# Routed attention and a cosine-gated MLP on one core: a remade instruction plan with fp32 turning of the first pairs, weights in sixteen paced pieces, and a last tile in halves

## Chip, cores, metric

One core of a Trainium2 chip. The time is the device time of one execution in microseconds (us). A run is called slow when it lies over 1.5% above the fastest of the same kernel on that chip; verdicts use the other runs, which are called fast.

## The reference, cut

```python
# q, k, v: (4, 8, 768, 64); centroids: (8, 16, 64); w_in: (512, 2048); w_out: (2048, 512)
q_assign = argmax(q_n @ c_n.T);  k_assign = argmax(k_n @ c_n.T)      # rows normalised
scores = where(q_assign[..., :, None] == k_assign[..., None, :], q @ k.T / 8, -1e9)
attn_out = softmax(scores) @ v
x = attn_out.transpose(0, 2, 1, 3).reshape(3072, 512)
h = x @ w_in
return (h * cos(h)) @ w_out                                           # (3072, 512) fp32
```

The kernel works on 16 pairs of heads (0 to 15, four for each batch entry). For each pair, scores of 80 rows (64 of q or k, 16 of the one-hot cluster) go through 9 exps. The MLP of a batch entry fills the time of later pairs. The first four pairs have no MLP work beside them. PE is TensorE, ACT ScalarE, DVE VectorE, POOL GpSimd and SP SyncE; "turned" means transposed, and a "move" is the 24 KB transfer that puts one-hot rows in their place.

## The kernel before

The program first collects operations with booked durations (`pl.add`), then a small planner simulates five engines and the DMA and emits each engine's instructions in the order found. On the chip each engine runs its own list strictly in that order. The planner's times exist only in the plan; what really holds an engine is a data dependence or a full buffer.

```python
# Plan.run, before: each queue's first transfer moves, and moving ones share the DMA by weights pk
heads = {}
for f in flying:
    heads.setdefault(f[0].ring, f)
moving = [f for f in heads.values() if f[2] <= t]
tot = sum(f[0].pk for f in moving)
...
# after routing: where a one-hot row goes. Pairs 0 and 1 (NHEAD = 2): turned by PE, copied by ACT and DVE.
if p < NHEAD:
    for hh in range(2):
        onehot_head(p, hh, ...)
else:
    onehot_pair(p, at + 5)      # turned, then four 24 KB moves: DMA copies into rows 64 to 79 of qkT
...
who, eng = ("SP", nc.sync) if p < HPB else ("POOL", nc.gpsimd)       # HPB = 4
pl.add(who, ..., lambda ...: eng.dma_start(out=turned(p, a, hh)[D:KDIM, :], in_=ohT[...]), ...)
...
def weight_ops():
    for ft in range(NFT):                                             # 4 loads of 512 KB
        pl.add("POOL", 0.6, lambda ft=ft: nc.gpsimd.dma_start(out=w_in_sb[:, ft, :], in_=w_in_r[ft]),
               -90 + 0.1 * ft, writes=[("w_in", ft)], ..., after=gate["hi", 2, 0], name="w_in")
    for f in range(0, NFPT, 4):                                       # 4 loads of 512 KB
        pl.add("POOL", 0.6, lambda f=f: nc.gpsimd.dma_start(out=w_out_sb[:, f:f + 4, :], ...),
               -50, writes=[("w_out", f // 4)], ..., after=gate["mv", 4], name="w_out")
    pl.add("SP", 0.45, lambda: nc.sync.dma_start(out=pace, in_=w_out_sb[0:1, NFPT - 1, 0:1]), 0,
           reads=[("w_out", 3)], writes=["pace"], ..., name="pace")
    gate["pace"] = (pl.ops[-1],)          # later loads and DMA transposes stand behind it on SP
```

The last line matters below. SP issues the loads of q, k and v and the large DMA transposes (`qkT<-stg`). Its two-byte transfer `pace` reads w_out, so SP **really waits** for the last w_out load, and everything behind it on SP's list waits too.

The softmax here doesn't subtract the row's maximum and nothing guards it: scores larger than these inputs give would overflow.

Of the kernel before, what the change touches and what calls it, by code (L numbers as in the profile page):

```python
# [19 lines left out]
class Op:  # L20
    __slots__ = ("eng", "occ", "lat", "work", "fn", "at", "nb", "deps", "outs", "left",
                 "take", "free", "table", "done", "idx", "name", "start", "ring", "pk", "urgent", "todo", "eta")


class Plan:
# [3 lines left out]
    HELD = 0.8  # L29
    OWN = {"PE": 0.0, "DVE": 0.11, "ACT": 0.0, "POOL": 0.08, "SP": 0.0}  # L30
    TABLE = 1.45
    urgent = False

# [5 lines left out]
    def add(self, eng, occ, fn, at, reads=(), writes=(), lat=0.13, work=0.0, nb=0.0, take=None,  # L39
            free=None, table=None, after=(), ring=None, pk=0.065, name="",  # L40
            urgent=False):
        o = Op()
        o.eng, o.occ, o.fn, o.at, o.lat, o.work, o.nb = eng, occ, fn, at, lat, work, nb
        o.take, o.free, o.table, o.name, o.ring, o.pk = take, free, table, name, ring, pk
# [18 lines left out]
    def run(self, stop=None):  # L63
# [9 lines left out]
        flying = []  # L73
# [14 lines left out]
        while n_left:  # L88
# [28 lines left out]
            for e in engines:  # L117
                if busy[e] > t or not ready[e] or any(
                        f[0].eng == e and f[0].pk < 0.02 and f[1] > self.HELD for f in flying):
                    continue  # L120
                back = []
                got = None
                while ready[e]:
                    item = heapq.heappop(ready[e])
                    o = item[2]
                    if o.take is not None and not free[o.take[0]]:
                        back.append(item)
                        continue
                    if (e == "DVE" or o.name == "warm") and any(x.at < o.at and x.eta < t + o.occ - 0.05 for x in soon[e]):
                        back.append(item)  # L130
                        break
                    got = o
                    break
# [8 lines left out]
                occ = o.occ  # L142
                if o.table is not None and o.table != table:
# [11 lines left out]
                if o.ring:  # L155
                    flying.append([o, o.work, t + min(occ, 0.45) + (1.1 if o.ring == "SW" else 0.8)])
# [3 lines left out]
            heads = {}  # L160
            for f in flying:
                heads.setdefault(f[0].ring, f)
            heads = list(heads.values())
            moving = [f for f in heads if f[2] <= t]
            tot = sum(f[0].pk for f in moving)
            when = [x for x in busy.values() if x > t] + [f[2] for f in heads if f[2] > t]
            when += [q[0][0] for q in (ends, coming) if q]
            for f in moving:
                when.append(t + f[1] * tot / f[0].pk)
                if f[1] > self.HELD and f[0].pk < 0.02:  # L170
                    when.append(t + (f[1] - self.HELD) * tot / f[0].pk)
# [6 lines left out]
            for f in moving:  # L178
                f[1] -= step * f[0].pk / tot
                if f[1] <= 1e-5:  # L180
                    heapq.heappush(ends, (t + 0.75, f[0].idx, f[0], False))
                    flying.remove(f)
        self.span = t
        return order


@with_exitstack
def kernel(
# [31 lines left out]
    NPE = 4  # L220
# [5 lines left out]

    NNAT, NSTG, NQK, NOH, NV, NE, NG, NO = 3, 2, 4, 2, 4, 4, 4, 3
    NACC = 4
    RT = 8
    BLOCKED = (HPB - 1,)  # L230
    NHEAD = 2
# [8 lines left out]
    ident = sb.tile([P, P], FP16, name="ident")  # L240
    oh_mul = sb.tile([P, 1], FP32, name="oh_mul")
# [25 lines left out]
    pl = Plan({"one": 4})  # L267
# [30 lines left out]
    def consts_ops():  # L298
        def mk_ident():
            make_identity(nc, ident)  # L300
        pl.add("POOL", 0.6, mk_ident, -90, writes=["ident"], name="ident")
# [21 lines left out]
    def warm_ops(n):  # L323
        for i in range(n):
            pl.add("PE", 0.43 if i < 8 else 0.216, lambda: nc.tensor.matmul(  # L325
                bank("warm"), lhsT=warm_z[:, 0:P], rhs=warm_z, start=True, stop=True),
                400 + i if i else -100, reads=["warm_z"] + ([] if i == 0 else [("warm", 0)]),
                writes=[("warm", i)], take=("one", "warm") if i == 0 else None,
                free="warm" if i == n - 1 else None, name="warm", lat=0.0)
# [8 lines left out]
    cn_s = sb.tile([HC, D], FP32, name="cn_s")  # L338
    cn_hl = sb.tile([HC, 2, 2, D], FP16, name="cn_hl")
    cside = sb.tile([P, H, 2, NCL], FP16, name="cside")  # L340

    def centroid_ops():
        V = nc.vector
        at = -120
        pl.add("ACT", 0.42, lambda: nc.scalar.dma_start(out=cn_raw, in_=centroids.rearrange("h c d -> (h c) d")),
               -149.9, writes=["cn_raw"], work=0.1, ring="ACT", name="ld cn")
        pl.add("DVE", 0.22, lambda: V.tensor_mul(cn_sq, cn_raw, cn_raw), at, ["cn_raw"], ["cn_sq"], name="cn")
        pl.add("DVE", 0.22, lambda: V.reduce_sum(out=cn_n2, in_=cn_sq, axis=AX.X), at, ["cn_sq"], ["cn_n2"], name="cn")
        pl.add("ACT", 0.2, lambda: nc.scalar.activation(out=cn_nrm, in_=cn_n2, func=AF.Sqrt), at,
               ["cn_n2"], ["cn_nrm"], table="sqrt", name="cn")  # L350
        pl.add("DVE", 0.15, lambda: V.tensor_scalar_add(cn_nrm, cn_nrm, 1e-6), at, ["cn_nrm"], ["cn_nrm2"], name="cn")
        pl.add("DVE", 0.16, lambda: V.reciprocal(cn_rcp, cn_nrm), at, ["cn_nrm2"], ["cn_rcp"], name="cn")
        pl.add("POOL", 0.3, lambda: nc.gpsimd.tensor_scalar(out=cn_s, in0=cn_raw, scalar1=cn_rcp, scalar2=ASCALE,
                                                    op0=ALU.mult, op1=ALU.mult), at, ["cn_rcp"], ["cn_s"], name="cn")
        wide = cn_s.rearrange("r (o d) -> r o d", o=1).to_broadcast([HC, 2, D])
        pl.add("POOL", 0.3, lambda: nc.gpsimd.tensor_copy(out=cn_hl[:, 0], in_=wide), at, ["cn_s"], ["cn_h"], name="cn")
# [505 lines left out]
```

## Time and profile before

| | us |
|---|---|
| median of 3 runs | 313.98 (313.61 to 314.23) |
| span of the profiled run | 312.2 |
| PE work at the measured peak rates | 287.7 |
| first exp starts / 36th exp (the last of pairs 0 to 3) ends | 15.84 / 54.28 |
| last matmul ends to end of span | 3.9 |

What to keep in mind for later are the transfers. These are rows of the page's sixth part for the kernel before: what is loaded, from which queue, how often, size of each, and the median time from issue to landing.

```profile
w_in_sb<-in_moe_w_in_dram POOLq DMA_DIRECT2D x4, 512.0 KB, 9.6
w_out_sb<-in_moe_w_out_dram POOLq DMA_DIRECT2D x4, 512.0 KB, 9.2
qkT<-ohT POOLq DMA_DIRECT2D x48, 24.0 KB, 2.9
```

And from its chain of waits (start, duration, what) the first large DMA transpose, that of pair 4, with no weight load in flight:

```profile
37.48 6.12 DMA qkT<-stg
```

Weights take 9 to 10 us to land in the median; w_in has landed by 29.7 and is first read at 53.7. The transpose takes 6.1 us (the later ones, also with no weight in flight, 5.6 to 9.8) and the one-hot moves 3 us, and PE stands behind both.

### The profile page before, as it was taken

What the parts mean: (1) busy time and instruction counts of PE and PEld (TensorE: products, weight loads), DVE (VectorE), ACT (ScalarE), POOL (GpSimd) and SP (SyncE); (2) the same over time, 40 slices, a digit from 0 to 9 for tenths busy, and PEclk for the clock granted to TensorE, in tenths of its full rate; (3) what the DMA queues carried; (4) which work ended last, traced back from release to release, by engine and by line L of the source; (5) the groups of instructions that cost most, each with busy time, mean ns of one, the idle gap of its engine ahead of it and who ended that gap; (6) DMA issues with size and microseconds to landing.
All of it is one profiled execution on the core that took longest, in us unless ns stands there. A gap on an engine that the chain in (4) does not pass through costs nothing.

```text
span 312.2 us, 7990 instructions
## 1 busy us (share of the span) xinstructions
PE 300.7 (96%) x3380; PEld 212.1 (68%) x3380; DVE 186.8 (60%) x362; ACT 213.7 (68%) x230; POOL 59.5 (19%) x114
## 2 busy tenths in 40 slices
PE   8899999999999799999999999999999999999995
PEld 3568877747785566788875567598866567776642
DVE  4789987513899467679872528677651123554431
ACT  5699999599249799875459996954479984533110
POOL 3793003401042232023132110032210100000000
PEclk9999999999999999999999999999999999999999
DMA  7897771797969999998545398972412202001012
GB/s 247 310 207 185 267 154 29 130 153 179 230 209 172 196 244 253 236 222 154 108 130 152 99 201 266 159 183 42 105 41 86 55 5 62 34 2 67 16 54 101
DMA packets 75254, 44.86 MB, mean 144 GB/s; under 512 B 56402, under 2 KB 71634, under 8 KB 75218
## 3 DMA queue, kind: packets, MB, share of 16 engines
q1 hardware_dynamic: 70706, 38.74, 50.2%
q0 software_dynamic: 4224, 5.38, 9.1%
q8 instruction: 26, 0.43, 0.6%
q10 hardware_dynamic: 288, 0.23, 0.2%
q14 instruction: 10, 0.08, 0.1%
HBM read 27.30 MB, written 6.29 MB: 108 GB/s over the span
## 4 chain that ended last, share of the span: by engine, by line
PE 76%; DMA 11%; ACT 6%; DVE 4%; POOL 1%; issue 1%; ACTq 0%; POOLq 0%; DVEq 0%
PE one L764 23%; PE big L728 23%; PE big L613 14%; PE one L679 8%; ACT e L619 5%; DMA qkT<-stg 5%; DMA w_out_sb<-in_moe_w_out_dram 3%; PE one L325 2%; DMA qkT<-ohT 2%; PE one L488 2%; PE one L460 2%; PE one L483 1%; DMA ohT<-oh 1%; DVE g L742 1%; POOL qkT L577 1%
## 5 line engine op out<-in xcount | busy, mean ns | idle before, releaser
L619 ACT ACTIVATE e<-big 128x1024 f16<-128x1024 f32 x144 | 139.6, 1022 | 12.0 <-PE big L613 10.9
L764 PE MATMUL one<-w_out_sb,g 128*128 128x512 f16 x384 | 108.3, 379 | 0.3 <-DMA w_out_sb<-in_moe_w_out_dram 0.3
L728 PE MATMUL big<-xt,w_in_sb 128*128 128x256 f16 x768 | 93.6, 272 | 0.8 <-DVE g L742 0.5
L736 ACT ACTIVATE cos_t<-big 128x1024 f16<-128x1024 f32 x48 | 49.1, 1023 | 65.8 <-PE big L728 63.7
L613 PE MATMUL big<-qkT 80*128 80x256 f16 (+1 forms) x396 | 85.2, 320 | 2.3 <-DMA qkT<-ohT 1.8
L728 PEld LDWEIGHTS <-w_in_sb 128*128 128x128 f16 x768 | 73.8, 98 | 17.1 <-issue 1.3
L742 DVE TENSOR_TENSOR g<-big,cos_t 128x1024 f16<-128x1024 f32 x48 | 58.6, 1222 | 32.3 <-ACT cos_t L736 32.0
L679 PEld LDWEIGHTS <-e 128*128 128x128 f16 x1080 | 45.7, 98 | 11.6
L764 PEld LDWEIGHTS <-g 128*128 128x128 f16 x384 | 36.3, 97 | 25.0 <-issue 0.7
L613 PEld LDWEIGHTS <-qkT 80*128 80x128 f16 x396 | 34.7, 97 | 25.5 <-DMA qkT<-ohT 2.3
L679 PE MATMUL one<-v_ext,e 128*128 128x65 f16 x1080 | 49.2, 194 | 0.0
L577 POOL DMA_DIRECT2D qkT<-ohT x48 | 23.7, 496 | 100.1 <-DMA ohT<-oh 46.2
L431 DVE SCALAR_TENSOR_TENSOR stg<-qk_nat,stg 128x384 f16<-128x384 f32 x64 | 34.9, 562 | 0.2
L771 DVE COPY o_sb<-one 128x512 f32<-128x512 f32 x24 | 16.5, 688 | 29.8 <-PE one L764 29.7
L396 POOL CAST v_ext<-v_nat 128x384 f16<-128x384 f32 x32 | 17.0, 562 | 75.7 <-DMA v_nat<-in_v_dram 75.6
L690 DVE RECIPROCAL recip<-one 128x6 f32<-128x6 f32 x30 | 5.8, 192 | 38.4 <-PE one L679 38.2
L427 DVE TENSOR_SCALAR stg<-qk_nat 128x384 f16<-128x384 f32 x48 | 16.5, 359 | 3.5 <-DMA qk_nat<-in_q_dram 2.8
L692 DVE TENSOR_TENSOR av_stage<-one,recip 128x384 f16<-128x384 f32 x30 | 16.6, 552 | 0.4
L502 DVE TENSOR_REDUCE csum<-one 128x192 f32<-128x384 f32 x24 | 12.9, 551 | 4.0 <-PE one L488 3.8
L488 PEld LDWEIGHTS <-qkT 128*128 128x128 f16 x288 | 10.9, 96 | 3.6 <-DMA qkT<-stg 1.6
L488 PE MATMUL one<-cside,qkT 128*128 128x32 f16 x288 | 11.5, 177 | 0.9 <-DMA qkT<-stg 0.9
L591 ACT ACT_TABLE_LOAD x9 | 11.5, 1283 | 0.2
(62 smaller groups left out, 129.7 us busy)
## 6 DMA issues: line engine op xcount, KB each, us to landing
v_nat<-in_v_dram SPq DMA_DIRECT2D x16, 384.0 KB, 4.5
out_dram<-o_sb SPq DMA_DIRECT2D x24, 256.0 KB, 2.2
qk_nat<-in_q_dram SPq DMA_DIRECT2D x15, 384.0 KB, 4.8
qk_nat<-in_k_dram SPq DMA_DIRECT2D x15, 384.0 KB, 5.3
w_in_sb<-in_moe_w_in_dram POOLq DMA_DIRECT2D x4, 512.0 KB, 9.6
w_out_sb<-in_moe_w_out_dram POOLq DMA_DIRECT2D x4, 512.0 KB, 9.2
qkT<-ohT POOLq DMA_DIRECT2D x48, 24.0 KB, 2.9
qk_nat<-in_q_dram SPq DMA_DIRECT2D x2, 192.0 KB, 3.1
```

Of the source, the lines that this page charges most:

```text
L396: pl.add("POOL", 0.5, lambda hh=hh: nc.gpsimd.tensor_copy(out=v_b[p % NV][:, hh, :, 0:D], in_=vnat_b[p % 2][:, hh]), (pair_at(p) - 2 if p ...
L431: pl.add("DVE", 0.476, lambda src=src, dst=dst: nc.vector.scalar_tensor_tensor(out=dst[:, :, 1, :], in0=src, scalar=ASCALE, in1=dst[:, :, ...
L488: nc.tensor.matmul(cs[:, a, t].rearrange("p i c -> p (i c)"), lhsT=turned(p, a, hh)[:, t * P:(t + 1) * P], rhs=cside[:, h].rearrange("p i ...
L577: pl.add(who, 0.61 if who == "SP" else 0.5, lambda hh=hh, a=a, r0=r0, eng=eng: eng.dma_start(out=turned(p, a, hh)[D:KDIM, :], in_=ohT[r0:r ...
L613: nc.tensor.matmul(big[i][:, x:x + w], lhsT=turned(p, 1, hh)[0:KDIM, jt * P:(jt + 1) * P], rhs=turned(p, 0, hh)[0:KDIM, col:col + w], star ...
L619: pl.add("ACT", 0.94, lambda i=i, c=c: nc.scalar.activation(out=e_b[p % (NE // 2)][:, c * CW:(c + 1) * CW], in_=big[i], func=AF.Exp, scale ...
L679: nc.tensor.matmul(av[:, i, :], lhsT=e_b[p % (NE // 2)][:, x:x + P], rhs=v_b[p % NV][:, hh, j, :], start=(j == 0), stop=(j == NT - 1))
L692: pl.add("DVE", 0.475, lambda av=av, r=r, hh=hh: nc.vector.tensor_tensor(out=av_t[:, :, hh, :], in0=av()[:, :, 0:D], in1=r.to_broadcast([P ...
L728: nc.tensor.matmul(bg[:, fi], lhsT=w_in_sb[:, ft, f * P:(f + 1) * P], rhs=xt_b[b % 2][:, ft, tg * TG:(tg + 1) * TG], start=(ft == 0), stop ...
L736: pl.add("ACT", 0.94, lambda bg=bg, cs=cs: nc.scalar.activation(out=cs, in_=bg, func=AF.Sin, bias=PI_HALF, scale=1.0), n, reads=[("big", i ...
L742: pl.add("DVE", 1.135, lambda bg=bg, cs=cs, c=c, slot=slot: nc.vector.tensor_tensor(out=g_b[slot][:, c * FQ:(c + 1) * FQ, :], in0=bg, in1= ...
L764: nc.tensor.matmul(bank(key), lhsT=g_b[slot][:, f, i * P:(i + 1) * P], rhs=w_out_sb[:, f, :], start=(f == 0), stop=(f == NFPT - 1))
```

## The change

The intent: start earlier (pairs 0 and 1 are turned while still fp32, and split into high and low halves on the way out of PSUM), let the planner see the DMA as one line that serves one transfer after another, search for better priorities in that planner (table `TUNE`, some 250 entries), bring the weights in 16 pieces of 256 KB that are let out only as earlier ones land, and shorten the end with a last tile in two halves.

```diff
 # the planner
-flying.append([o, o.work, t + min(occ, 0.45) + (1.1 if o.ring == "SW" else 0.8)])
+dma = max(dma, t + self.PRE[o.ring]) + o.work          # PRE: SP, ACT 1.5; SW (POOL) 0.85
+heapq.heappush(ends, (dma + self.POST, o.idx, o, False))   # POST 0.65
+TUNE = {'E0': -2.9, 'E1': -17.2, ... 'mv1.01': 'POOL', ... 'mv3.00': 'POOL', 'mv3.01': 'POOL', ...}
 ...
 # the head
-NPE = 4
-NHEAD = 2
+N32, NPE, NOT, NX, NSP = 2, 4, 5, 4, 5
+NHEAD = pick("nhead", 1, 1, 2)                         # TUNE has no "nhead": it is 1
+nc.tensor.transpose(out=bank(key)[:, u * P:(u + 1) * P], in_=nat[:, a, hh, 2 * u:2 * u + 2]..., identity=ident32)
+nc.scalar.mul(st[:, a, hh, 0], src(), ASCALE)          # split out of PSUM
-pl.add("ACT", 0.42, lambda: nc.scalar.dma_start(out=cn_raw, in_=centroids...), ...)
+pl.add("POOL", 0.6, lambda: nc.gpsimd.dma_start(out=cn_raw, in_=centroids...), ...)
 ...
 # one-hot moves
-who, eng = ("SP", nc.sync) if p < HPB else ("POOL", nc.gpsimd)
+who = pick(f"mv{p}.{hh}{a}", "SP" if p < NSP else "POOL", "SP", "POOL")
+eng = nc.sync if who == "SP" else nc.gpsimd
 ...
 # weights
+def weight_pieces(name, pieces, at, after):
+    for i, (key, dst, src) in enumerate(pieces):
+        if i > 1:
+            old = pieces[i - 2]
+            pl.add("POOL", 0.12, lambda old=old: nc.gpsimd.tensor_copy(out=pace, in_=old[1][0:1, 0, 0:1]), ...,
+                   reads=[old[0]], ..., name="pace")
+        pl.add("POOL", 0.77, lambda dst=dst, src=src: nc.gpsimd.dma_start(out=dst, in_=src), ..., work=1.5, bulk=True)
-pl.add("SP", 0.45, lambda: nc.sync.dma_start(out=pace, in_=w_out_sb[0:1, NFPT - 1, 0:1]), ...)
 # 'w_out_after': 'w_in' in TUNE: w_out follows w_in's last piece instead of pair 4's moves
 ...
 # the end
+cols = ((0, DM),) if (b, t) != (B - 1, NT - 1) else ((0, DM // 2), (DM // 2, DM))
```

(`...` marks cuts in the code. The whole diff is some 740 lines, mostly the remade head and the table.)

## The prediction

> **What bounds the kernel now.** I read the page first (engines, then groups), then the chain of waits, then busy time by stretches of 8 us, then the timeline of the first 20 us on each engine. Engine totals from the page:
>
> ```profile
> PE 300.7 (96%) x3380; PEld 212.1 (68%) x3380; DVE 186.8 (60%) x362; ACT 213.7 (68%) x230; POOL 59.5 (19%) x114
> PE 76%; DMA 11%; ACT 6%; DVE 4%; POOL 1%; issue 1%; ACTq 0%; POOLq 0%; DVEq 0%
> ```
>
> PE (TensorE) is busy 96%, but that alone does not say that it runs at its rate, because the ends of matmuls are modelled. So I took start-to-start times from merged pieces of the chain, where matmuls of one shape run back to back:
>
> ```profile
> 76.95 8.34 DMA qkT<-stg
> ...
> 139.03 3.49 PE big L728 x32
> ...
> 296.84 11.45 PE one L764 x53
> 308.32 0.69 DVE o_sb L771
> ```
>
> 512 columns: 11.45/53 = 0.216 us; 256 columns: 3.49/32 = 0.109 us. In the same way 24 value matmuls of 65 columns take 0.77 us (0.032 each), 24 routing matmuls 0.59 us (0.0246), six 128-column transposes 0.34 us (0.056). Times the counts of the groups: w_out 384 x 0.216 = 82.9; w_in 768 x 0.109 = 83.7; scores 180 x 0.216 + 216 x 0.109 = 62.4; values 1152 x 0.032 = 36.9; routing 288 x 0.0246 + 192 x 0.025 = 11.9; transposes 176 x 0.056 = 9.9. The sum is **287.7 us of work that PE must do**, without the 24 dummy matmuls (warm_z). The span is 312.2, so PE loses 24.5 us, and only that can be won. Where it is lost shows in the stretches (after the times: length, then busy us of PE, PEld, DVE, ACT, POOL, then clock, DMA share, GB/s):
>
> ```profile
> 0.00:8.00 8.00, 6.82 (x36) 2.95 (x37) 3.87 (x13) 4.46 (x9) 2.99 (x17) 1.00 0.76 250
> 8.00:16.00 8.00, 6.92 (x108) 4.55 (x107) 5.72 (x14) 5.68 (x10) 6.06 (x7) 1.00 0.85 296
> ...
> 48.00:56.00 8.00, 7.25 (x110) 5.97 (x107) 5.00 (x16) 7.41 (x8) 2.85 (x6) 1.00 0.17 36
> ...
> 80.00:88.00 8.00, 7.32 (x110) 6.31 (x108) 6.74 (x14) 3.07 (x3) 0.00 (x0) 1.00 1.18 246
> ...
> 104.00:112.00 8.00, 6.21 (x95) 4.28 (x95) 4.03 (x8) 5.93 (x7) 2.91 (x6) 1.00 1.06 245
> ...
> 112.00:120.00 8.00, 8.00 (x105) 5.34 (x104) 5.56 (x15) 7.95 (x9) 3.33 (x6) 1.00 1.01 225
> ```
>
> By counting matmuls per stretch at the rates above I get four parts of the loss. (a) **Head**: the first score matmul starts at 14.88 and only about 4.3 us of needed work ran before it (50 transposes, 60 routing matmuls); 10.6 us lost. (b) From 14.9 to 54.3, where ACT (ScalarE) ends the 36th exp of the first four pairs, some 3.5 us. (c) From 54 to 136 some 5 us, of which 1.8 is one wait for a moved one-hot row and 0.7 one wait for a DMA transpose; both fall where the DMA share is about 1. (d) **Tail**: 312.2 - 308.3 = 3.9 us after the last matmul. The rest is rounding and small gaps. From 136 to 308 PE has no measurable gap: all that it had to do there it did at its rate. The waits of PE say the same:
>
> ```profile
> PE big L613 <- DMA qkT<-ohT: 1.8, 1, 1.8
> PE one L488 <- DMA qkT<-stg: 0.9, 2, 0.7
> ```
>
> **What the Trainium skill says.** "TensorE: Matmul & The Clock Gate", section "Wait — 56ns, not 53.3ns?": warm start-to-start is 55.6 ns at 128 columns and 215.7 at 512, with a floor of about 25 ns for small ones. The trace agrees (56, 216, 24.6), so PE cannot go faster than the sum above. The same page, Part 1, says that the first 3.4 us or so of activity run at half clock; the trace agrees in kind: the first eleven dummies take 4.61 us, 0.42 each. "PSUM — Partial Sum Buffer", section "Specifications (TRN2)": transposes write the input dtype uncast, which is what makes turning fp32 first and splitting afterwards possible; nothing before shows it. The first page's "Weight-path perf modes — Fast Weight Load (FWL) and DoubleRow" says that the fast weight load is off for FP32; so an fp32 transpose may cost more than its 0.056 us fp16 sister. No row of this trace has one; the author's plan books 0.13 us, an assumption that I carry with doubt.
>
> **The change part by part.**
>
> *Pairs 0 and 1 as fp32.* Before: load, split into hi and lo (ACT 0.51, DVE 0.56), transpose, copy out of PSUM (0.56 or 0.79), routing, argmax, transpose of one-hots, copies, scores. After: load, transpose, split from PSUM, routing directly from the split tiles with a padded centroid table; the copy of q and k into place stands beside routing. PE: -48 x 0.056 + 24 x 0.13 (est.) = +0.4 us in all; the 96 routing matmuls grow from 16 to 32 columns, both at the floor. In the trace DVE (VectorE) stood still until 4.75 for the centroids, while ACT had three hi parts ready by 5.10; the change sends their load through POOL (GpSimd) and their squares to ACT. Working along DVE's new order from about 4.3: centroids and splitting six short and four 0.5 us steps, one placing copy, tables 0.7, so the first argmax at about 8.5 instead of 10.67; then two reductions and compares to 10.1, one-hot transposes, ACT copies 0.79 each with DVE's between them; first exp near 12.8 instead of 15.84. Estimate for the head: **-3.0**. Between the exps of pair 0 ACT also had three copies of 0.79 and keeps one split of 0.51.
>
> *DMA as one line, and the search.* Nothing is computed less; orders, buffers' times and which queue moves a one-hot row (27 through SP instead of 8) change. It can win only from (b) and (c), 8.5 us. Half seems fair: the kernel before came from a similar plan without search and lost little, and a searched order fits the plan better than the chip. **-4.0**.
>
> *Weights in 16 paced pieces.* w_out was issued at 54 and landed at 67.7; it is in the chain for 10.7 us, but PE waited just 0.3 for it. Earlier w_out lets out-matmuls fill gaps in (c); counted above. The cost is six plus six 1x1 copies on POOL, which is 19% busy.
>
> *Small moves.* Pair 4's one-hots go to PE (+6 transposes, +0.3); pair 5's and 11's output turning swap places (0).
>
> *Last tile in halves.* Twice 16 matmuls of 256 columns cost 16 x (0.218 - 0.216), nothing. The last copy is 128 columns on ACT and DVE each instead of 512 (0.69 us to about 0.25), and the last store is 128 KB instead of 256 KB. Tail 3.9 to 3.2: **-0.7**.
>
> Sum: -3.0 - 4.0 - 0.7 + 0.4 + 0.3 = -7.0 on the span; I keep +0.3 for new stalls of an order that has no slack left: 313.98 - 6.7 = **307.3 us**.
>
> **The rivals.** *First: the head's gain is swallowed.* ACT does 36 exps in about 0.955 us each, 34.4 us, and PE has about as much work there (scores 15.7, values 9, turning and routing some 9). If loads of pairs 2 to 4 now share the DMA with earlier weights, pairs arrive late and the exps wait. For it: pairs 0 to 4 and the weights are about 14 MB, and the trace's best stretches move some 300 GB/s, so some 47 us of the first 55 are needed. Against: pieces are released only when the line is short. Then 310 to 311. *Second: fp32 transposes are slow* (four times the fp16 cost in weights and columns): 12 of them lie ahead of the first exp; +1 to +2, so 309. *Third: the searched order works as planned* and PE runs from about 12 us to the end without loss: 288.4 of work, some 8 lost in the head, 3.2 in the tail, 1.5 between: span 301, time 303. Against it: one late transfer stalls an in-order PE. *Fourth: PE-bound anyway*, gaps only move: only head and tail show, 310.5.
>
> **Range and chances.** 307.3, with 303.8 to 310.6 as eight in ten. The 2% line lies at 307.7, almost on my number, so the two outcomes are nearly even; slower needs new stalls of over 13 us, for which I see no ground. Faster 0.54, same 0.44, slower 0.02.
>
> **What would show it.** First exp at 12.3 to 13.3 (before 15.84). The 36th exp ends at 48 to 50.5 (before 54.3). Time from the last matmul to the end 3.0 to 3.4. PE's needed work 288.4 by the same rates; the wait of PE for the one-hot move gone or under 0.7; PE busy 97 to 98% of the span. From 136 us on no gap, as before: the gain must all be there by then. An fp32 transpose under 0.15 us start to start. The prediction is wrong if the first exp is no earlier, if PE waits over 3 us in sum for DMA, or if a gap opens in the second half.

## The result

| | before | after |
|---|---|---|
| median, us (4 runs each, same rounds) | 313.8 | 326.45 |
| lowest to highest | 313.05 to 314.23 | 325.01 to 330.21 |
| span of the profiled run | 312.2 | 324.5 |
| first exp starts | 15.84 | 14.24 |
| 36th exp ends | 54.28 | 65.94 |
| from there to the end | 257.9 | 258.6 |
| mean clock granted to PE | 1.0 | 0.967 |

The change made the kernel slower: the ratio is 1.039, 95% interval 1.035 to 1.043. All ratios here are the mean time of one kernel's fast runs over the mean of the other's fast runs of the same rounds, so they are not quite the ratios of the medians.

The table already places the loss. The first exp is 1.6 us earlier, the 36th is 11.7 us later, and from there both kernels take the same time within a microsecond. The rows "36th exp ends" and "from there" are used for every experiment below.

The page of the kernel after, first the engine totals, then busy tenths and granted clock (tenths of full speed) in 40 slices of 8.1 us:

```profile
PE 305.1 (94%) x3365; PEld 218.4 (67%) x3365; DVE 184.8 (57%) x360; ACT 210.3 (65%) x228; POOL 64.3 (20%) x124
...
PE   7985967999998999999799999999999999999995
...
PEclk9996985799999999999999999999999999999999
```

Before, PE was 96% busy and the clock row was all nines. Now slices 4, 6, 7 and 8 are damaged. Busy time *rose* (305.1 against 300.7) although PE's needed work is the same by the prediction's rates (288.2 against 287.7): at a lower clock the same matmul is busy for longer (the first five matmuls of a pair's scores take 1.86 us at 28.01, at clock 0.50, and 1.03 us at 14.88 in the kernel before). So busy time hides the loss. The stretches show it, in the columns of the prediction (length, busy us and count of PE, PEld, DVE, ACT, POOL, then clock, DMA share, GB/s):

```profile
24.00:32.00 8.00, 3.99 (x38) 2.79 (x39) 2.54 (x7) 1.94 (x2) 4.43 (x8) 0.65 0.86 176
...
40.00:48.00 8.00, 5.37 (x103) 4.27 (x102) 4.91 (x14) 6.10 (x7) 1.91 (x5) 0.93 1.03 220
48.00:56.00 8.00, 6.03 (x57) 4.41 (x55) 3.59 (x9) 2.59 (x3) 2.59 (x5) 0.50 1.20 202
56.00:64.00 8.00, 8.00 (x130) 7.20 (x128) 3.47 (x9) 6.41 (x7) 4.35 (x9) 0.71 0.79 121
```

Where the kernel before ran 161 matmuls in 24 to 32, this one ran 38. Counting matmuls by start and shape, times the prediction's rates, PE lost about 16.4 us of 40 between 24 and 64, against 3.5 before. Three gaps make 9.1 us of it (4.5, 2.6 and 2.0); the rest is for the most part work at half clock, which the trace shows from 26.5 to 33.3 and from 46.9 to 60.6. Another 3 us are lost between 136 and 160, where the prediction saw no gap (two waits of 1.14 and 1.45 us, for a product of DVE and for a DMA transpose); 1.8 us are won back between 64 and 136.

PE's longest waits of the kernel after (total, times, longest):

```profile
PE big L770 <- issue: 4.5, 1, 4.5
PE one L609 <- DMA qkT<-stg: 3.1, 3, 1.4
PE one L836 <- POOL v_ext L452: 2.6, 1, 2.6
PE big L770 <- DMA qkT<-ohT: 2.0, 1, 2.0
```

The three waits for DMA transposes come at 82.8, 105.6 and 159.6, after the weights; between 24 and 64 PE waited for the other three rows alone. "issue" names no releaser. That wait ends at 28.01, at the first scores of pair 1:

```profile
28.01 1.86 PE L770 MATMUL big<-qkT 80*128 80x512 f16 x5 [4.53 <-issue]
```

POOL's timeline of the kernel after shows what it did in that time (start, duration, instruction, and in brackets the idle time before it and what ended that):

```profile
20.90 0.76 POOL L955 DMA_DIRECT2D w_in_sb<-in_moe_w_in_dram  x1
21.67 0.53 POOL L734 DMA_DIRECT2D qkT<-ohT  x1
23.08 0.18 POOL L952 COPY pace<-w_in_sb 1x1 f16<-1x1 f16 x1 [0.88 <-DMA w_in_sb<-in_moe_w_in_dram]
...
27.85 0.18 POOL L952 COPY pace<-w_in_sb 1x1 f16<-1x1 f16 x1 [3.14 <-DMA w_in_sb<-in_moe_w_in_dram]
...
45.46 0.19 POOL L952 COPY pace<-w_in_sb 1x1 f16<-1x1 f16 x1 [5.49 <-DMA w_in_sb<-in_moe_w_in_dram]
...
47.01 0.96 POOL L452 CAST v_ext<-v_nat 128x384 f16<-128x384 f32 x2
```

Two things are to be seen. A 24 KB one-hot move of pair 1 (L734, at 21.67) was issued on POOL's queue behind weight pieces of 256 KB. It took 6.25 us and landed at 27.92, the last of the pair's four, and PE started 0.09 us later: this move is what ended the wait. And the pace copies stand still for 3.14 and 5.49 us until a piece has landed; POOL runs in order, so the cast of pair 2's values at 47.01, whose data were there, stood still with them. PE's first value matmul of that pair started at 47.57, after the 2.6 us in the table of waits.

The rows of the transfers that answer to those of before:

```profile
w_in_sb<-in_moe_w_in_dram POOLq DMA_DIRECT2D x8, 256.0 KB, 6.7
w_out_sb<-in_moe_w_out_dram POOLq DMA_DIRECT2D x8, 256.0 KB, 4.4
qkT<-ohT POOLq DMA_DIRECT2D x33, 24.0 KB, 3.7
qkT<-ohT SPq DMA_DIRECT2D x27, 24.0 KB, 3.2
```

The plan books a w_in piece at 0.85 + 1.5 + 0.65 = 3.0 us from issue to landing; it took 6.7. It books a move at 1.5 (on POOL 0.85) + 0.17 + 0.65, so at most 2.3 us when the line is empty; the median is 3.2 to 3.7, and the moves that ended PE's waits at 28.01 and 54.02 took 6.25 and 5.57. The transpose of pair 4, booked at 5.65 us, was issued at 44.71 and landed 10.3 us later. An order made from the booked landings can turn such an error into a wait; which it did is read from the waits above.

### The profile page after: what moved, and what is told of

Same layout as the page of the kernel before. It is cut to its first block, busy times and chain, and to the rows that moved or that the text cites. A ratio compares the mean times of both kernels' runs of the same rounds, so it can differ in the third digit from the quotient of the medians.

```text
span 324.5 us, 7970 instructions
## 1 busy us (share of the span) xinstructions
PE 305.1 (94%) x3365; PEld 218.4 (67%) x3365; DVE 184.8 (57%) x360; ACT 210.3 (65%) x228; POOL 64.3 (20%) x124
## 4 chain that ended last, share of the span: by engine, by line
PE 69%; DMA 18%; POOL 3%; ACT 3%; DVE 3%; issue 3%; SPq 0%; POOLq 0%; DVEq 0%; ACTq 0%
PE one L923 23%; PE big L885 19%; PE big L770 15%; PE one L836 8%; DMA qkT<-stg 7%; DMA w_in_sb<-in_moe_w_in_dram 4%; PE one L609 2%; DMA qkT<-ohT 2%; POOL stg L499 2%; ACT e L776 1%; DMA ohT<-oh 1%; DMA cn_raw<-in_centroids_dram 1%; DMA qk_nat<-in_q_dram 1%; DVE g L899 1%; DMA qk_nat<-in_k_dram 1%
## 5 line engine op out<-in xcount | busy, mean ns | idle before, releaser
L923 PE MATMUL one<-w_out_sb,g 128*128 128x512 f16 (+1 forms) x400 | 108.2, 370 | 0.0
L770 PE MATMUL big<-qkT 80*128 80x256 f16 (+1 forms) x396 | 89.3, 333 | 6.6 <-issue 4.5
L885 PE MATMUL big<-xt,w_in_sb 128*128 128x256 f16 x768 | 91.8, 272 | 1.2 <-DVE g L899 1.1
L893 ACT ACTIVATE cos_t<-big 128x1024 f16<-128x1024 f32 x48 | 49.1, 1023 | 67.7 <-PE big L885 64.2
L836 PEld LDWEIGHTS <-e 128*128 128x128 f16 x1080 | 48.7, 101 | 16.6 <-issue 3.1
L836 PE MATMUL one<-v_ext,e 128*128 128x65 f16 x1080 | 52.8, 198 | 2.6 <-POOL v_ext L452 2.6
L923 PEld LDWEIGHTS <-g 128*128 128x128 f16 x400 | 37.9, 97 | 22.7
L734 POOL DMA_DIRECT2D qkT<-ohT x33 | 16.3, 496 | 106.2 <-DMA ohT<-oh 32.5
L936 DVE COPY o_sb<-one 128x512 f32<-128x512 f32 (+2 forms) x25 | 16.6, 662 | 36.3 <-PE one L923 34.5
L504 DVE SCALAR_TENSOR_TENSOR stg<-qk_nat,stg 128x384 f16<-128x384 f32 x56 | 29.9, 556 | 0.6 <-POOL stg L499 0.4
L499 POOL TENSOR_SCALAR stg<-qk_nat 128x384 f16<-128x384 f32 x9 | 10.8, 1199 | 8.1 <-DMA qk_nat<-in_k_dram 6.0
```

What stands on the lines that cost most here:

```text
L499: "POOL": lambda src=src, dst=dst: nc.gpsimd.tensor_scalar_mul(dst[:, :, 0, :], src, ASCALE),
L504: pl.add("DVE", 0.476, lambda src=src, dst=dst: nc.vector.scalar_tensor_tensor(out=dst[:, :, 1, :], in0=src, scalar=ASCALE, in1=dst[:, :, ...
L770: nc.tensor.matmul(big[i][:, x:x + w], lhsT=turned(p, 1, hh)[0:KDIM, jt * P:(jt + 1) * P], rhs=turned(p, 0, hh)[0:KDIM, col:col + w], star ...
L836: nc.tensor.matmul(av[:, i, :], lhsT=e_b[p % (NE // 2)][:, x:x + P], rhs=v_b[p % NV][:, hh, tile_of(p // HPB, j), :], start=(j == 0), stop ...
L885: nc.tensor.matmul(bg[:, fi], lhsT=w_in_sb[:, ft, f * P:(f + 1) * P], rhs=xt_b[b % 2][:, ft, tg * TG:(tg + 1) * TG], start=(ft == 0), stop ...
L893: pl.add("ACT", 0.94, lambda bg=bg, cs=cs: nc.scalar.activation(out=cs, in_=bg, func=AF.Sin, bias=PI_HALF, scale=1.0), n, reads=[("big", i ...
```

## Experiments

Eighteen kernels ran, in five groups that each share a chip and the runs of the kernel before. All gave correct results. "36th" is the end of the 36th exp, "rest" the span from there to the end, both from the profiled run (before: 54.3 and 257.9, profiled in the first measurement alone; beside the experiments the median of the kernel before was 1.0 to 1.6 us longer, so differences of that size in these two columns say nothing). The planner makes the order anew in e5 to e12 and e16 to e18; e1 to e4 and e13 to e15 keep it.

**Group 1: cure one wait.** e1 takes away what the pace copies do and leaves the order as it was; e2 issues all one-hot moves of pairs 1 to 3 from SP; e3 does both; e4 changes nothing but keeps PE's clock up with 41 dummy matmuls at the places of the gaps (20, 12 and 9).

```diff
 # e1, e3
-lambda old=old: nc.gpsimd.tensor_copy(out=pace, in_=old[1][0:1, 0, 0:1])
+lambda: None
 # e2, e3
-eng = nc.sync if who == "SP" else nc.gpsimd
+eng = nc.sync if who == "SP" or p < HPB else nc.gpsimd
 # e4
+for _ in range(dummies):
+    nc.tensor.matmul(big[i][:, 0:512], lhsT=warm_z[:, 0:P], rhs=warm_z, start=True, stop=True)
```

> The changed kernel with its instruction order kept and only the twelve 1x1 pace copies on POOL left out, so POOL never waits for a weight piece to land. Theory A (POOL's in-order queue: a pace copy waits for a weight piece and holds up pair 1's placing copies, pair 2's value casts and pair 3's one-hot moves behind it): the 2.6 us wait of PE for the value cast at 45 us goes and the pieces go out early; the 4.5 us gap at 23.5 stays or not depending on theory B; time 317 to 322. Theory B (the one-hot move of pair 1 that is issued from POOL sits behind a weight piece in the one software DMA queue): with pieces issued still earlier the gap at 23.5 stays at 4 us or grows; time 322 or more. If the gaps have nothing to do with POOL: 326.

> The changed kernel with the order kept, but the one-hot moves of pairs 1 to 3 that the search put on POOL are issued from SP. Theory B (software queue behind weight pieces): the 4.5 us gap before pair 1's scores at 23.5 falls to under 1.5 us, and the 2.0 us wait for the move of pair 3 at 52 falls too; the 2.6 us wait for the value cast (held by a pace copy) stays; time 317 to 321, clock above 0.98. Theory A alone (POOL's queue held by pace copies): pair 1's placing copies are what PE waits for, so the gap stays near 4 us; time 325 to 327.

> Both edits: no pace copies, and the one-hot moves of pairs 1 to 3 from SP. If A and B together are the cause of the loss up to 64 us, PE waits under 3 us in sum before 64 us, the granted clock is 1.0 after the start, and the time is 310 to 314 (what remains is the 3 us loss near 152 us and the ordinary ones); if another cause (sheer DMA bandwidth) is behind the late pieces, gaps of 5 us or more remain before 64 us and the time is 318 or more.

> The changed kernel with dummy matmuls put in PE's order where it stalled: 20 ahead of pair 1's scores, 12 ahead of pair 2's values, 9 ahead of pair 3's scores, so that PE is busy in the same waits and its clock should not drop. It tells the cost of the lowered clock from the cost of the waits. If the clock itself costs: granted clock at least 0.99, and time 321 to 323 (half-rate work between 28 and 33 and between 46 and 62 us cost about 4 us). If in these stretches transfers set the pace anyway, the waits only grow and the time stays at 325 to 327 with a clock near 1.

| | median | before | ratio (95%) | clock | 36th | rest |
|---|---|---|---|---|---|---|
| e1 | 330.82 | 315.24 | 1.053 (1.046 to 1.060) | 0.963 | 70.6 | 258.5 |
| e2 | 328.58 | 315.24 | 1.046 (1.039 to 1.053) | 0.958 | 68.6 | 260.0 |
| e3 | 325.18 | 315.24 | 1.038 (1.028 to 1.047) | 0.976 | 64.2 | 258.5 |
| e4 | 323.98 | 315.24 | 1.030 (1.024 to 1.036) | 0.998 | 60.8 | 259.1 |

Neither single cure won, and e1 lost: by its time it lies in its branch for theory B (whose gap of 4 us did not come), e2 above both of its branches, e3 in the one for another cause. The gap before pair 1's scores fell from 4.5 to 2.9, 2.1 and 2.8 us and in each of the three ended 0.09 us after one of the pair's moves landed (at 25.96, 25.13 and 26.11), whatever the waits are labelled: from SP such a move still took 4.2 to 5.4 us. And PE now stood at pair 4's transpose, which took 19.6 us in e1 and 17.9 in e2 (PE waited 8.9 and 7.9 us for it). In e3 no wait for POOL is left among PE's longest, yet the time is that of the change: the waits are for DMA (transposes 7.2 us in four, moves 4.8 us in three). From the chain of waits of e3:

```profile
44.09 12.98 DMA qkT<-stg
```

Here the transpose took 13.0 us: without pace copies four w_out pieces were issued from 42.63 to 44.77 and were in flight beside it. e4 restored the clock in its profiled run (0.984 to 0.995 in the others) and won about 0.9% of the time, between its two branches; PE's loss between 24 and 64 fell from 16.4 to 11.4 us. So the lost clock is a real but smaller share; the larger part of the loss stayed with PE at full clock.

**Group 2: what of the change is to blame?** e5 drops the table of the search; e6 turns pair 1's one-hots by PE again; e7 puts the weights back as before (four loads of 512 KB each, at their old places, no pace copies, but without SP's wait) and keeps all else; e8 is e7 without the search and with pair 1 as in e6.

```diff
 # e5, e8
-pl.tune = TUNE
+pl.tune = {}
 # e6, e8
-NHEAD = pick("nhead", 1, 1, 2);  RSPLIT = (0,)
+NHEAD = 2;  RSPLIT = (0, 1)
 # e7, e8: weight_ops and weight_out_ops issue the loads of the kernel before
+for x in (f, f + 1): nc.gpsimd.dma_start(out=w_in_sb[:, x, :], in_=w_in_r[:, x, :])     # after hi of pair 2
+nc.gpsimd.dma_start(out=w_out_sb[:, f:f + 4, :], in_=w_out_r[:, f:f + 4, :])            # after moves of pair 4
```

> The changed kernel with the table of searched shifts emptied: same operations, same DMA account in the plan, the order by the default priorities. Theory C (the search packed consumers up to transfers that the plan books too short: one-hot moves at 2.3 us against 5.4 measured, weight pieces at 3.0 against 4 to 10, the first big transpose at 5.7 against 10 to 13): without the search PE waits under 4 us in sum before 64 us; time 312 to 317. Theory D (the parts themselves: pair 1's one-hot rows now go by DMA, weights start and share the DMA early, pace copies on POOL): gaps of 5 us or more before 64 us stay and the time is 320 or more.

> The changed kernel, searched shifts kept, but pair 1's one-hot rows go into place by PE transposes and ACT and DVE copies as in the kernel before, not by four small DMAs (the plan's order is made anew). If the DMA moves of pair 1 are the cause of the first gap: PE's gap near 23.5 us is under 1 us, pair 1's scores start before 24.5 us, and 3 to 6 us are won against the changed kernel: 320 to 323. If pair 1's placing copies on POOL behind a pace copy hold it: the gap stays near 4 us and the time is 325 to 328.

> The changed kernel, searched shifts kept, but the weights loaded as in the kernel before: four 512 KB loads of w_in after the first split of pair 2, four of w_out after the moves of pair 4, no pace copies (order made anew). If early weights and pacing take the DMA and POOL from the pairs: PE waits under 4 us before 64 us, time 315 to 320. If the searched order is at odds with the chip whatever the weights do: 324 or more.

> The fp32 turning, the DMA account and the split last tile alone: no search, weights as before, pair 1's one-hot rows by PE. Theory of a good head: first exp at 14.0 to 14.5 us against 15.84, and no gap that the kernel before does not have: 311 to 314, ratio 0.990 to 1.0. If the DMA account in the plan by itself makes a worse order: 317 or more.

| | median | before | ratio (95%) | 36th | rest |
|---|---|---|---|---|---|
| e5 | 331.27 | 315.44 | 1.047 (1.039 to 1.055) | 70.2 | 260.4 |
| e6 | 330.63 | 315.44 | none: of 4 runs only one, 323.85, counts as fast | 61.5 | 260.5 |
| e7 | 317.59 | 315.44 | 1.005 (1.002 to 1.008), 18 of 20 runs fast | 53.5 | 262.3 |
| e8 | 322.58 | 315.44 | 1.018 (1.010 to 1.027) | 62.6 | 258.8 |

The search is not the cause by itself: without it the kernel is no faster. e7 is the clearest result, and as expected. With the weights as before, nearly all of the loss is gone, in a planner that is otherwise the new one. Its 36th exp ends no later than before; but in this profile the rest takes 4.4 us longer (over its fast runs the whole loss is 1.5 us), so it still does not win. e8 shows that the old weights are not all: it loses 1.8%, nearly all of it before the 36th exp, with waits of 3.4 us for moves and 2.7 for transposes. e6 scattered over 3% in four runs and is inconclusive.

**Group 3: which weights?** e9 takes back only w_in, e10 only w_out. e11 is the other way round: the kernel *before* with the sixteen paced pieces alone (SP's wait goes with them, as in the change). e12 is the kernel before with the change's head, centroids and last tile.

```diff
 # e9: w_in as in e7.   e10: w_out as in e7.
 # e11, in the kernel before: weight_ops as in the change
-pl.add("SP", 0.45, lambda: nc.sync.dma_start(out=pace, in_=w_out_sb[0:1, NFPT - 1, 0:1]), ...)
+weight_pieces("w_in", pieces, -90, gate["hi", 2, 0]);  weight_pieces("w_out", pieces, -50, gate["mv", 4])
 # e12: the change with the planner, priorities, weights and moves of the kernel before
```

> The changed kernel, searched shifts kept, but only w_in is loaded as in the kernel before (four loads of 512 KB, full 8 KB rows, right after the first split of pair 2); w_out stays in eight paced pieces after w_in (order made anew). If w_in's pieces, spread from 15 to 50 us through POOL and the software queue, are the larger share of the loss: 316 to 320. If it is w_out, which now comes before pair 4's transpose and pair 3's moves instead of after pair 4's moves: 323 to 327.

> The mirror of the last: w_in in eight paced pieces as changed, w_out as in the kernel before. If w_in's pieces are the larger share: 322 to 327 with gaps before pair 1's scores near 23 us and clock below 0.99. If w_out is: 316 to 320.

> The kernel before with one part of the change alone: weights in 16 paced pieces, released by the same events as its own loads. If paced pieces as such hurt (POOL held by pace copies, moves behind pieces in the software queue), PE waits over 4 us more than before between 20 and 75 us: 318 to 325. If they hurt only together with the new order, in which pair 1's scores hang on four small moves: 313 to 316.

> The kernel before (its plan with the old DMA account, its weights, its load order, no search) with the fp32 turning of pairs 0 and 1, the centroids through ACT and the last tile in halves. If the head's gain is real and reaches the end: first exp at 13.8 to 14.6 us against 15.84, 311.5 to 313.5, ratio 0.990 to 0.997. If it is eaten in the ACT-bound stage that follows: ratio 0.998 to 1.005.

| | median | before | ratio (95%) | 36th | rest |
|---|---|---|---|---|---|
| e9 | 334.03 | 314.79 | 1.061 (1.053 to 1.069) | 59.5 | 274.8 |
| e10 | 328.13 | 314.79 | 1.041 (1.035 to 1.047) | 64.6 | 261.5 |
| e11 | 332.8 | 314.79 | 1.058 (1.050 to 1.066) | 55.8 | 275.8 |
| e12 | 317.92 | 314.79 | 1.011 (1.005 to 1.017) | 56.6 | 257.8 |

Neither half alone suffices, and e9 to e12 came out above all that was expected of them. e10 has w_out late and keeps the w_in pieces. Its longest PE waits:

```profile
PE big L770 <- DMA qkT<-ohT: 4.2, 2, 2.6
PE big L770 <- issue: 3.5, 1, 3.5
PE one L836 <- POOL v_ext L452: 2.6, 1, 2.6
```

The waits before the 36th exp are those of the change: pair 1's move from POOL (it landed at 26.64, PE started at 26.73), the cast behind a pace copy, a move of pair 3. So they belong to the w_in pieces. e9, the mirror, has 1.1 us of such waits left; PE waits 9.4 us in four for transposes, and most of its loss comes after the 36th exp, which is only 5.2 us late.

e11 shows that the paced pieces hurt the old order as well, though in another place: its 36th exp is only 1.6 us late. The longest of its PE waits:

```profile
PE one L764 <- DMA w_out_sb<-in_moe_w_out_dram: 9.8, 1, 9.8
```

And from the chain of e11 the transpose of pair 4, which stood at almost the same time in the kernel before:

```profile
37.65 10.49 DMA qkT<-stg
```

Pacing w_out behind pair 4's moves made it arrive when it was already needed, hence one wait of 9.8 us. The transpose beside w_in pieces took 10.5 us instead of 6.1. e12 says that the new head with the new last tile gains nothing at the end, and loses 1.1%: the first exp is 1.6 us earlier, but the 36th is 2.3 us later. (Its expectation speaks of centroids through ACT; the run kept the change's load through POOL.) Its order was remade with booked times of the kernel before, so this is the head in that plan, not the head as such.

**Group 4: size, wait, burst.** e13 is the kernel before with each weight load cut in two pieces of 256 KB in the change's shape, at the same places and unpaced. e14 is the kernel before without SP's wait. e15 is the change with all eight w_in pieces issued at the first one's place and all eight w_out pieces at the third's, with no pace copies and the moves from SP. e16 is e7 with pair 1's one-hots by PE.

```diff
 # e13, in the kernel before
-nc.gpsimd.dma_start(out=w_out_sb[:, f:f + 4, :], in_=w_out_r[:, f:f + 4, :])
+[nc.gpsimd.dma_start(out=w_out_sb[:, x:x + 2, :], in_=w_out_r[:, x:x + 2, :]) for x in (f, f + 2)]     # w_in alike
 # e14, in the kernel before
-lambda: nc.sync.dma_start(out=pace, in_=w_out_sb[0:1, NFPT - 1, 0:1])
+lambda: None
 # e15, in the change
-lambda dst=dst, src=src: nc.gpsimd.dma_start(out=dst, in_=src)
+lambda i=i: [nc.gpsimd.dma_start(out=d, in_=s) for _, d, s in pieces] if i == (0 if name == "w_in" else 2) else None
 # e16: the edits of e7, and NHEAD and RSPLIT of e6
```

> The kernel before with its order and times of issue, each of its eight 512 KB weight loads cut into the two pieces of 256 KB that the change uses (rows of 2 KB of w_in or w_out read, 1 KB written), no pacing. If the shape of the pieces costs: w_in lands over 4 us later than before, PE waits more, 317 or more. If the shape is harmless: 313 to 315.5, ratio within 0.5%.

> The kernel before without the tiny transfer by which SP waits for the last of w_out before it issues the next transposes and loads (instruction order kept). The change has no such wait on SP. If that wait protects the weights from transposes: w_out lands several us after 67.7, PE waits for it, 317 or more; if it only costs SP time: 311 to 314.

> The changed kernel's order on every engine and its 256 KB pieces, but all eight of w_in issued where the first was (15 us), all of w_out where the third was, no pace copies, and pair 1 to 3's moves from SP. If the spread of the pieces over the time of the moves is the cause, not their shape: w_in lands before 30 us, PE waits under 4 us before 64 us, 315 to 320, near the run with the old weights (317.6). If the early w_in burst only delays pair 1's moves more: a gap of over 4 us before pair 1's scores and 323 or more.

> The searched shifts and the fp32 head, weights as in the kernel before, and pair 1's one-hot rows by PE instead of DMA moves. The run with the old weights still had PE wait for pair 1's moves at 20 to 26 us (scores of pair 1 at 25.9). If that is what is left: pair 1's scores start by 23.5 and the time is 311 to 314.5, ratio 0.99 to 1.0; if the remade order opens other waits: 316 to 320.

| | median | before | ratio (95%) | 36th | rest |
|---|---|---|---|---|---|
| e13 | 318.94 | 315.06 | 1.002 (0.998 to 1.006), 8 of 20 runs fast | 55.2 | 257.4 |
| e14 | 318.77 | 315.06 | 1.013 (1.006 to 1.020) | 54.6 | 261.6 |
| e15 | 331.34 | 315.06 | 1.052 (1.041 to 1.063) | 71.9 | 258.0 |
| e16 | 326.68 | 315.06 | 1.036 (1.027 to 1.046) | 52.6 | 273.1 |

Small pieces as such cost little. The ratio of e13 rests on the fast runs alone; twelve of its twenty lay between 318 and 322, so the true cost is somewhere between nothing and 1.2%. e14 says what SP's two-byte wait was worth: 1.3%, the branch in which it protects w_out. Without it two transposes ran beside w_out and took 10.8 and 18.9 us; w_out landed in 13.6 us in the median instead of 9.2, and PE waited 2.9 us for it. In e15 eight w_out pieces were issued from 44.70 on, and its chain has:

```profile
47.58 16.85 DMA qkT<-stg
```

So pair 4's transpose took 6.1 us (no weight beside it), 10.3 (the change), 13.0 (e3), 16.9 (e15), 17.9 (e2) and 19.6 (e1). Beside weights it is longer each time, but not in the order of their number: e2 had four pieces in flight, e15 eight. The Trainium skill ("DMA: Bandwidth & Descriptors", section "Issuing engines are not separate DMA queues") says that transfers issued by different engines end up on the same 16 DMA engines and interleave. The trace agrees: the transpose comes from SP's queue and the weights from POOL's, and the second queue gave no shelter. e16 was meant as the best version and is not: it has the earliest 36th exp of all, and then loses 15 us more than before in the rest; over the whole run PE waits 5.2 us for moves and 4.9 for transposes. It differs from e7 in pair 1's one-hots alone and lies 3% from it, so an order made anew can by itself move the time by that much. With the old weights the runs lie at 1.005, 1.018, 1.024 and 1.036 (e7, e8, e18, e16), with paced pieces of both weights at 1.039 to 1.058 (the change, e5, e11): the direction is shown, the size in e7 rests on one order.

**Group 5: the causes together.** No cure alone had brought the ratio under 1.03. e17 applies three to the change: no pace copies, moves of pairs 1 to 3 from SP, w_out as before. The small w_in pieces, the search and the head stay. e18 is e7 with SP's real wait put back and with the moves from SP.

```diff
 # e17: the edits of e3, and w_out as in e10.   e18: the edits of e7, the moves as in e2, and
+pl.add("SP", 0.45, lambda: nc.sync.dma_start(out=pace, in_=w_out_sb[0:1, NFPT - 1, 0:1]), 0, reads=[("w_out", 14)], ...)
```

> The change with three cures at once: its w_in pieces without pace copies, the one-hot moves of pairs 1 to 3 from SP, and w_out in four loads after pair 4's moves as before. Theory (the loss is POOL's in-order pace copies, moves behind weight pieces on POOL's queue, and w_out beside the DMA transposes): the waits of PE for pair 1's move and pair 2's values go, the first big transpose takes under 8 us, 315 to 319 us, ratio at most 1.015. Rival (small w_in pieces or the searched order lose by themselves): 323 or more, ratio over 1.025.

> The change with the weight loads of the kernel before at their old places, SP's real wait for the last w_out load put back ahead of the later DMA transposes, and the moves of pairs 1 to 3 from SP. Theory (head, search and small moves gain a little once the weights do no harm): 311 to 314 us, ratio 0.99 to 1.0, the only version that could beat the kernel before. Rival (the fp32 head and the search gain nothing at the end): 315 to 319, ratio 1.005 to 1.02.

| | median | before | ratio (95%) | clock | 36th | rest |
|---|---|---|---|---|---|---|
| e17 | 319.74 | 315.33 | 1.016 (1.011 to 1.021) | 0.984 | 56.4 | 262.6 |
| e18 | 322.33 | 315.33 | 1.024 (1.019 to 1.029) | 0.984 | 58.6 | 262.7 |

e17 takes away more than half of the loss (3.9% to 1.6%), just outside the top of what was expected, and below the rival. In the contested part it goes further: the 36th exp ends at 56.4 instead of 65.9, so 9.6 of the 11.7 us are back. Between 24 and 64 PE loses about 7.3 us by the same count, against 16.4. What is left of PE's longest waits in e17:

```profile
PE big L770 <- POOL qkT L582: 2.3, 1, 2.3
PE big L770 <- DVE stg L500: 2.3, 1, 2.3
PE one L609 <- DMA qkT<-stg: 1.3, 1, 1.3
```

The labels of the first two mislead. POOL's last placing copy of pair 1 had ended at 25.12; PE started at 25.84, again 0.09 us after a move of pair 1 had landed, which SP had issued 4.9 us before, beside w_in pieces. The second ends at 96.89, 0.05 us after a move that took 4.86 us. So what is left is the same wait as in the change, half the size, and issuing the move from SP does not do away with it. The transpose of pair 4 is at 7.2 us; the next one, issued into w_out, took 16.9, but PE had MLP work. The rest is 4.7 us longer than before, as in e7, e10 and e14 (3.6 to 4.4), which also issue w_out after pair 4's moves without SP's wait. For e14, where nothing else differs from the kernel before, the missing wait is the cause. For the others it is not shown: e8 issues w_out in the same way and has a rest of 258.8, and e18, with the wait back, still has 262.7. In e18 SP issued nothing but eight moves between 19.79 and 28.58, and the loads behind them came late; e18 came out above both of its branches. All these orders were remade by the planner, and what costs them the last 4 to 5 us stays open.

No version beat the kernel before, so the head's earlier start was turned into time in none of the runs.

## Why the prediction was wrong

Its text is above; these are its steps in order.

**What bounds the kernel: right.** PE's needed work stayed 288 us, and all that happened was loss.

**Head, -3.0: right in kind, half the size, and no gain at the end.** The first exp came at 14.24, not 12.8. DVE should have begun on the centroids at "about 4.3". Their load through POOL landed so late that ACT squared them at 5.41 and DVE started at 6.02; the first argmax came at 10.30, not 8.5. And in e12 these 1.6 us were gone by the 36th exp.

**fp32 transposes, +0.4: right.** At full clock they start 0.11 to 0.17 us after one another; the first nine, where a dummy of 512 columns took 0.43 (half clock), 0.21 to 0.24. The second rival, four times 0.056, is out at full clock.

**DMA account and search, -4.0: wrong.** No run shows a gain from it. I wrote that "a searched order fits the plan better than the chip", and then gave it half of a possible gain with no term for the misfit. The change lost about 12.9 us more between 24 and 64 than the kernel before. But the search alone did not do it: e5 loses as much without it, and with the old weights the same search is at 1.005 (e7). (Two readings of the prediction are off: by start times part (b) of the loss is 4.7 us, not 3.5, and w_out was issued from 55.4 on and had landed at 70.1, not 54 and 67.7.)

**Weights, nothing: this is the step that failed.** The prediction put it so: "The cost is six plus six 1x1 copies on POOL, which is 19% busy." It costed the copies by their duration, 0.18 us, and POOL by its mean share, and put down nothing for what the pieces do to the transfers beside them. The runs show this in its place. One-hot moves beside the pieces took 6.25 and 5.57 us, and PE waited 4.5 and 2.0 us for them. The wait in front of a pace copy (5.49 us), which POOL hands on to everything behind it, cost PE 2.6 us. Behind these gaps PE worked at half clock; e4 puts about 0.9% on that. And it treated w_out's move to an earlier time as free, because PE had hardly waited for w_out; the question was what would be in flight beside it: pair 4's transpose took 10.3 us, which the other waits hid in the change, and up to 19.6 us in e1 to e3, where PE then waited 4.6 to 8.9 us for it. It also read the removed SP transfer as bookkeeping; e14 puts 1.3% on it in the kernel before. e7 shows the sum: with the weights, their places and pacing taken back, 3.9% becomes 0.5%; and e11 shows the reverse, 5.8% lost by the pieces in the kernel before. e17 takes pace copies, moves on POOL and early w_out away together and has 9.6 of 11.7 us back before the 36th exp, in an order made anew; the single shares are not shown.

**Small moves, +0.3: one missed.** The default of `NHEAD` went from 2 to 1, so pair 1's one-hot rows, copied by ACT and DVE before, became DMA moves, three on SP and one on POOL behind the w_in pieces. The 4.5 us gap ended with the landing of that one. The prediction told this nowhere, though it is one line of the diff. How much it costs alone is not shown: e6 was inconclusive and e16 lost elsewhere.

**Tail, -0.7: -0.2.** 3.7 us after the last matmul instead of 3.9. The timeline of the kernel after shows that the two quarter copies, meant to run side by side, ran one after the other. First ACT's:

```profile
320.82 0.27 ACT L933 COPY o_sb<-one 128x128 f32<-128x128 f32 x1 [8.73 <-PE one L923]
```

And DVE's, which stood idle for 1.62 us until ACT's was done:

```profile
321.12 0.29 DVE L936 COPY o_sb<-one 128x128 f32<-128x128 f32 x1 [1.62 <-ACT o_sb L933]
```

**The rivals.** The first (loads of pairs sharing the DMA with earlier weights) had the right place and resource, but saw only loads of pairs, put 3 us on it, and answered itself with "pieces are released only when the line is short". They are, but the transfers beside them still took two to three times what was booked, and the releasing cost PE 2.6 us more. The fourth rival and the third are out.

**Range and chances.** The prediction put the 36th exp at 48 to 50.5; it ended at 65.94. "Slower needs new stalls of over 13 us, for which I see no ground": the time is 19 us above the predicted one. Of its own warnings two came true: PE waited 5.5 us in sum for DMA by the labels (10.0 with the 4.5 us that a move ended), and a gap opened in the second half.

## What to carry to other kernels

Cost a wait on an in-order engine by what stands behind it, not by the engine's mean busy share; a tiny instruction that waits for a DMA can be as long as the DMA (5.49 us in front of a copy of 0.19 here). When a transfer that nobody waits for is moved, ask which latency-bound transfers it will now share the DMA with, and consider a real dependence, not a planned one, between the two (e14 shows its worth in the kernel before; e18, which put one back, shows none). Before believing a searched schedule, compare its booked landing times (3.0, 2.3 and 5.65 us here) with the trace's (6.7, 3.2 to 6.3, and 10.3). And where a wait has no label or one that ended long before, look for the transfer that landed just then.

## What the Trainium skill lacked or had wrong

- "TensorE: Matmul & The Clock Gate", section "HAM oscillation — how this bites in real kernels", gives the rule of no PE-idle gaps over some 3.4 us. The 4.5 us gap here agrees: from 26.5 to 33.3 us the clock was 0.50. But a gap of 2.6 us did it too, while one of 1.8 us in the kernel before did not. Stretches of 2 us in the kernel before, the first ending with its 1.8 us gap (columns as above; the clock is third from the end):

```profile
104.00:106.00 2.00, 0.21 (x2) 0.04 (x2) 0.00 (x0) 0.80 (x1) 0.00 (x0) 1.00 1.30 126
106.00:108.00 2.00, 2.00 (x27) 1.26 (x28) 0.69 (x1) 1.34 (x2) 0.51 (x2) 1.00 0.86 158
```

  And in the kernel after, the first lying wholly in its 2.6 us gap:

```profile
45.00:47.00 2.00, 0.00 (x0) 0.00 (x0) 0.87 (x3) 1.10 (x2) 0.92 (x2) 0.98 0.90 177
47.00:49.00 2.00, 1.43 (x20) 1.15 (x20) 0.00 (x0) 0.00 (x0) 2.00 (x6) 0.50 1.20 137
```

  Nor does length sort the shorter gaps: in e18 the clock fell to 0.50 at 27.9 and at 45.0, about half a microsecond after gaps of 1.8 and 1.7 us, and in e17 at 26.9, after one of 2.3 us; in e7 it held through one of 2.0 us (146.06 to 148.07). So staying below the rule did not keep the clock in this case; what decides there is not shown. In the kernel after the clock stayed at 0.50 from 46.9 to 60.6 us, through one further gap, of 2.0 us.
- "DMA: Bandwidth & Descriptors", section "Rules for kernel authors", says of correctness that "A transpose next to ordinary DMAs needs nothing". No page gives the price: pair 4's took 6.1 us with no weight in flight, and 10.3 to 19.6 us beside weight loads from POOL's queue (the change, e1 to e3, e15). The 261 GB/s that the same page gives for DMA transposes with a non-contiguous middle dimension (section "Latency and other measured facts") would move these 0.79 MB in 3.0 us, an estimate from that page; it leaves out the time before and after the bytes move, and from issue to landing the fastest took 5.5 us in the kernel after and 5.6 in the kernel before.
- A time for an fp32 transpose on PE is on no page that I found: 0.11 to 0.17 us start to start for 128 x 128 here at full clock, against 0.056 for fp16.
